# Plain products of ten pairs ahead of their sums in a Strassen-Winograd GeGLU kernel

## The chip, the cores and the metric

The kernel runs on one core of a Trainium2 chip. A core has a matrix engine (TensorE, "PE" in the profile, with its weight loads as "PEld"), a vector engine (VectorE, "DVE"), a scalar engine (ScalarE, "ACT"), a general engine (GpSimd, "POOL") and a queue engine (SyncE, "SP") that issues transfers, as ACT can too. They run side by side and wait for each other by semaphores. Each engine takes its own instructions strictly in order. The metric is the device time of one execution in microseconds; the time given is the median of the runs.

## The reference

```python
def setup_inputs():
    B, S, D, F = 1, 2048, 1024, 3584     # all bfloat16
    ...
def reference(x, w_gate, w_up, w_down):
    return (_gelu(x @ w_gate) * (x @ w_up)) @ w_down    # gelu: tanh form
```

2048 tokens with 1024 features are multiplied by two weight matrices of 1024 x 3584 ("gate" and "up"), GELU of the one is multiplied by the other, and the result goes through a third matrix of 3584 x 1024 ("down").

## The kernel before

**Tiling.** The tokens are taken in two halves of 1024 (`h` = 0, 1), each half in two blocks of 512 (`tb` = 0, 1). The 3584 hidden features are 28 tiles of 128; two neighbouring tiles make a pair, so there are 14 pairs. The contraction over 1024 is 8 steps of 128 (`KD`), in two halves of 4 (`KH`). One matmul multiplies a 128 x 128 weight block by 512 token columns into one PSUM bank of 128 x 512 fp32. There are eight banks, used two by two for gate (`j` = 0) and up (`j` = 1): `PB`, `VB`, `QB`, `RB`.

**Seven products for eight.** Done plainly, a pair needs 2 tiles x 2 blocks x 2 halves of K = 8 products of 4 matmuls, for gate and for up: 64 bf16 matmuls. The kernel uses Winograd's form of Strassen's scheme, seven products, 56 matmuls: M1 and M2 on plain bf16 operands, and M3 to M7 on sums held as fp32r. The sums of x (`t1` to `t4`, `b22`) are made once for a token half by `t_sum`; the sums of weights (`s1` to `s4`, `a22`) are made for each pair by `s_sum` (L388, on POOL; `a22` is a copy on ACT, L401). They have one place per name in `s_mem`, so a sum of the next pair can be made only when the product that reads the old one is over.

**`quads` (from L406)** runs pairs, mostly two at a time (a "couple"). It first does M1 for both pairs (4 matmuls for each of gate and up) and copies M1 to a second bank on ACT (L444), then adds M2 to the first bank: that is the plain output of the pair's first tile on the first token block, and goes through `gelu` (L286, ACT) and `mult` (L291, DVE) into `hT`. Then for each pair, 40 fp32r matmuls:

- M6 on bank Q (which holds M1), copied to bank R on ACT (L478); M5 on bank V, copied to SBUF as `m5` on ACT (L472);
- DVE adds `m5` to Q (L434); M7 goes on R, DVE adds R and `m5` into V (L434); V goes through GELU and product;
- M3 goes on Q, M4 on R, each followed by GELU and product.

`prep` puts the next pair's sums right behind the product that frees their place. `thens` is a table of further work hung between products ("start", "m5", "m7", "m3", "m4").

**Other work hung there in the first token half.** 42 staging steps (`stage_step`, L625, DVE, 128 x 512, SBUF to SBUF) prepare sums of the down weights, which go out to DRAM by SP; transposing loads of the next x (`stage_x`) go on SP; `s_down` (L670, DVE) makes sums of `hT` for the down projection; `t_down` (L600, DVE) makes sums of 1024 columns of the down weights. They stood spread over six couples.

**The start.** Pair 0 is done plainly on both blocks (`first_pair_units`, `part`, L267, 64 matmuls) while the rest of x and the weights land. The first four K steps of x are transposed by TensorE (L311), the others by transposing DMAs. Pair 1 runs alone in `quads` (with "early" in its `thens`: its successor's sums are made late), its own s3 sums on DVE (L386); then come six couples. In the second token half there are seven couples. After each half, `down_group` (L698) runs the down projection on two token groups, also with seven products; its first sums need `s_down` and `t_down` in time.

**Order.** Every instruction is tied to the one before it on its engine by `on`, so the order in the file is the order on each engine.

Of the kernel before, what the change touches and what calls it, by code (L numbers as in the profile page):

```python
# [34 lines left out]
def kernel(  # L35
# [8 lines left out]
    nc = tc.nc  # L44
# [52 lines left out]
    s_mem = shared_pool.tile([P, 4 * NS * P], F32R, name="s_mem")  # L97
# [44 lines left out]

    xs0 = w_mem[:, 4 * CH : 4 * CH + TSB * D].rearrange("p (a b) -> p a b", b=D)
    chunks = {}

    def new_chunk(key):
        c0 = 2 * CH * (key[1] % 2)
        chunks[key] = tuple(
            w_mem[:, c0 + j * CH : c0 + (j + 1) * CH].rearrange(
                "p (a b) -> p a b", b=FG  # L150
            )
            for j in range(2)
        )
# [33 lines left out]
    load_x0(0, sp, 0, 2)  # L187
    load_x0(0, act, 2, TSB)
    load_w(first, 0, 0, 2, sp, 0, FA)
    load_x0(1, act)  # L190
    load_w(first, 1, 0, 2, sp, 0, FA)
    load_w(first, 0, 2, 5, act, 0, FA)
    load_w(first, 1, 2, 5, sp, 0, FA)
# [20 lines left out]
    load_xT(xT, 0, 0, KH, KH + 1)  # L214
    behind_transpose = last_on["sp"]
    load_xT(xT, 0, 0, KH + 1, KH + 2)
    for j in range(2):
        load_w(first, j, 5, KD, act, 0, FA)
        tc.add_manual_dep(
            last_on["act"].ins,  # L220
            behind_transpose.ins.name,
            SCHED_DEP,
            reason="engine order",
        )
    act(nc.scalar.preload_act_table(ACT.Gelu_apprx_tanh))
    load_xT(xT, 0, 0, KH + 2, KD)
    for k0, k1 in ((0, 2), (2, KH), (KH, KD)):
        load_xT(xT, 0, 1, k0, k1)
    for j in range(2):
        load_w(first, j, 0, KD, sp, FA, FG)  # L230
    new_chunk((0, 1))
    for j in range(2):
        load_w((0, 1), j, 0, KD)
# [31 lines left out]
    def mm_gu(ps, w_sb, fi, tb, kd):  # L265
        pe(
            nc.tensor.matmul(  # L267
                ps[:],
                lhsT=w_sb[:, kd, fi * P : (fi + 1) * P],
                rhs=xT[tb][:, kd, :],  # L270
                start=(kd == 0),
                stop=(kd == KD - 1),
            )
        )

# [23 lines left out]
    def unit_out(hT, bset, fi, tb):  # L299
        mult(hT, gelu(banks[bset[0]]), banks[bset[1]], fi, tb)  # L300

    def transpose_x0(q):

        parts = [(2 * q, 0, 4), (2 * q + 1, 0, 4)]
        if q == 0:
            parts = [(0, 0, 2), (0, 2, 4), (1, 0, 4)]
        for n, (kd, ts0, ts1) in enumerate(parts):
            tp = banks[(PB + QB)[(2 * q + n) % 4]][:].bitcast(BF16)
# [14 lines left out]
    def part(held, tb, k0, k1, us=(0, 1), js=(0, 1)):  # L323
        for kd in range(k0, k1):
            for j in js:
                for u in us:
                    mm_gu(banks[held[u][j]], chunks[first][j], u, tb, kd)

    def first_pair_units(hT):

        held = (VB, RB)
        transpose_x0(0)
        warm(RB[1], TB // 2)
        part(held, 0, 0, KPQ, js=(0,))
        transpose_x0(1)
        part(held, 0, 0, KPQ, js=(1,))
        part(held, 0, KPQ, KD)
        t_sum("t1", 0, KH // 2)
        t_sum("t1", KH // 2, KH)
        for u in range(2):  # L340
            unit_out(hT, held[u], u, 0)
        held = (QB, PB)
        part(held, 1, 0, KH)
        t_sum("t2")
        t_sum("b22")
        t_sum("t3", 0, KH // 2)
        part(held, 1, KH, KD, (0,))
        unit_out(hT, held[0], 0, 1)
        t_sum("t3", KH // 2, KH)
        part(held, 1, KH, KD, (1,))  # L350
        unit_out(hT, held[1], 1, 1)
        for j in range(2):
            s_sum(0, 1, j, "s3", True, False)
        for name in ("s1", "s2", "s4"):
            for j in range(2):
                s_sum(0, 1, j, name)
# [5 lines left out]
    def block(key, j, i, kh):  # L362
        fi = 2 * (key[2] % PPG) + i
        w_sb = chunks[(key[0], key[2] // PPG)][j]
        return w_sb[:, half(kh), fi * P : (fi + 1) * P]
# [40 lines left out]
    def quads(hT, h, members, nxt, thens, m5_first):  # L406

        last = nxt is None
        run = []
        for n, pair in enumerate(members):  # L410
            after = (h, members[n + 1]) if n + 1 < len(members) else nxt
            first_ = (PB, RB)[n] if len(members) > 1 else VB
            run.append((pair, after, thens[n], first_, (QB, VB)[n]))
# [27 lines left out]
        for pair, _, _, first_, q_ in run:  # L441
# [4 lines left out]
        for pair, _, _, first_, _ in run:  # L446
# [8 lines left out]
        for n, (pair, after, then, _, Q_) in enumerate(run):  # L455
            f0 = 2 * pair
            ends = after is None
            eager = "early" in then

            def prep(j, name, after=after):  # L460
                if after is not None:
                    s_sum(after[0], after[1], j, name)
# [6 lines left out]
            def do_m5(j):  # L469
# [3 lines left out]
                if not eager:  # L473
                    prep(j, "s1")
# [6 lines left out]
            if eager:  # L481
                order = (do_m5, 0), (do_m5, 1), (do_m6, 0), (do_m6, 1)
            elif m5_first and n == 0:
# [7 lines left out]
            for j in range(2):  # L491
                add_m5(Q_[j], Q_[j], m5[j])
                if not eager:
                    prep(j, "s2")
            done(n, "m5")
            for j in range(2):
# [4 lines left out]
                if j == 0 and eager:  # L501
                    pool_behind_dve()
                    for name in ("s1", "s2"):
                        for i in range(2):
                            prep(i, name)
# [562 lines left out]
```

## Time and profile before

| | |
|---|---|
| median of 3 runs | 538.92 us (538.79 to 539.41) |
| span of the profiled execution | 537.4 us |
| TensorE clock granted | 1.00 throughout |
| POOL sums, L388 | 206 of 1.24, 1.34 and 1.20 us (three forms) |
| DVE steps, L625 from a step before | 28: 0.68 to 1.54 us, median 1.36 |
| DVE additions, L434, with PSUM | 108 of 0.69 us |
| DVE products, L291, with PSUM | 106 of 0.69 us |
| ACT GELU, L286 | 106 of 0.60 us |

The profile is one execution. Its first part gives busy time, share and instructions of each engine; the chain that ended last follows the work back from the last instruction, piece by piece, with start, length and line. A timeline line has start, length, engine, line, operation, tiles and count. "fp32r" and "f32" operands of a matmul are sums, "bf16" ones are plain.

The busy shares in 40 slices of 13.4 us (9 is 90% or more) show where each side engine has work:

```profile
DVE  2985868787876998989555353444444669979961
ACT  2555555556465329117465554656555551452280
POOL 0698696969696200000056494958677670000000
```

The first token half's pairs end at slice 13; slices 13 to 20 are its down projection.

### The profile page before, as it was taken

To read this page: it belongs to the slowest core of one execution; us is meant where nothing else is said; L and a number is where in the kernel's file an instruction comes from. 1 tells how busy PE (TensorE), PEld (TensorE's weight loads), DVE (VectorE), ACT (ScalarE), POOL (GpSimd) and SP (SyncE) were. 2 spreads that over 40 slices of the span, in tenths; PEclk is the share of its full clock that TensorE was granted. 3 is DMA by queue.
4 is the path that set the end of the run, shared out by engine and by line. 5 is a ranking of instruction groups with operands and counts; after the bars stand their busy time and mean duration, and the time that the engine had idled before them with its cause. 6 is when DMAs were issued, how large, how long until landed. Compare 5 with 4: busy or idle time off the path is not lost.

```text
span 537.4 us, 7033 instructions
## 1 busy us (share of the span) xinstructions
PE 533.6 (99%) x2388; PEld 379.2 (71%) x2388; DVE 367.6 (68%) x476; ACT 263.5 (49%) x447; POOL 252.2 (47%) x213
## 2 busy tenths in 40 slices
PE   9999999999999999999999999999999999999997
PEld 4568686867677686777768676776768686866866
DVE  2985868787876998989555353444444669979961
ACT  2555555556465329117465554656555551452280
POOL 0698696969696200000056494958677670000000
PEclk9999999999999999999999999999999999999999
DMA  9965759697623887788950413314040329677846
GB/s 220 329 199 134 267 164 304 182 320 199 229 53 143 318 288 243 243 292 292 329 168 12 145 62 97 110 48 154 3 156 22 136 84 337 228 237 250 292 143 212
DMA packets 92547, 102.70 MB, mean 191 GB/s; under 512 B 18656, under 2 KB 67424, under 8 KB 92512
## 3 DMA queue, kind: packets, MB, share of 16 engines
q1 hardware_dynamic: 69568, 80.23, 45.7%
q10 hardware_dynamic: 22944, 22.02, 13.2%
q8 instruction: 19, 0.31, 0.3%
q14 instruction: 16, 0.13, 0.1%
HBM read 85.98 MB, written 12.58 MB: 183 GB/s over the span
## 4 chain that ended last, share of the span: by engine, by line
PE 99%; ACT 0%; issue 0%
PE bank L418 63%; PE bank L698 33%; PE bank L267 3%; PE bank L202 1%; PE bank L311 0%; ACT o_sb L754 0%
## 5 line engine op out<-in xcount | busy, mean ns | idle before, releaser
L418 PE MATMUL bank<-t_mem,s_mem 128*128 128x512 f32 x1056 | 244.6, 392 | 0.0
L418 PEld LDWEIGHTS bank<-t_mem,s_mem 128*128 128x128 f32 x1056 | 198.1, 188 | 42.7 <-issue 0.2
L388 POOL TENSOR_TENSOR s_mem<-w_mem 128x512 fp32r<-128x512 bf16 x102 | 124.0, 1236 | 185.5 <-DMA out_dram<-o_sb 96.9
L698 PE MATMUL bank<-t_mem,s_mem 128*128 128x512 f32 (+1 forms) x548 | 127.2, 391 | 0.0
L698 PEld LDWEIGHTS bank<-t_mem,s_mem 128*128 128x128 f32 x548 | 102.5, 188 | 22.0
L291 DVE TENSOR_TENSOR hT<-w_mem,bank 128x512 bf16<-128x512 f32 x106 | 72.5, 687 | 66.5 <-PE bank L418 44.5
L434 DVE TENSOR_TENSOR bank<-bank,m 128x512 f32<-128x512 f32 x108 | 70.0, 694 | 56.1 <-ACT m L472 54.3
L418 PE MATMUL bank<-xT,w_mem 128*128 128x512 bf16 x432 | 95.7, 379 | 0.0
L286 ACT ACTIVATE w_mem<-bank 128x512 f32<-128x512 f32 x106 | 63.0, 597 | 64.1 <-DVE bank L434 34.8
L418 PEld LDWEIGHTS <-w_mem 128*128 128x128 bf16 x432 | 41.2, 98 | 51.3 <-issue 3.4
L388 POOL TENSOR_TENSOR s_mem<-w_mem,s_mem 128x512 fp32r<-128x512 bf16 x52 | 68.4, 1335 | 2.9 <-PE bank L418 2.9
L600 DVE TENSOR_TENSOR t_mem<-w_mem 128x1024 fp32r<-128x1024 bf16 x56 | 65.9, 1225 | 0.9 <-PE bank L418 0.9
L388 POOL TENSOR_TENSOR s_mem<-s_mem,w_mem 128x512 fp32r<-128x512 f32 x52 | 61.3, 1200 | 0.0
L401 ACT CAST s_mem<-w_mem 128x512 fp32r<-128x512 bf16 x54 | 33.2, 616 | 31.3 <-PE bank L418 30.1
L478 ACT COPY bank<-bank 128x512 f32<-128x512 f32 x54 | 30.8, 570 | 26.6 <-PE bank L418 26.6
L670 DVE TENSOR_TENSOR s_mem<-hT 128x512 fp32r<-128x512 bf16 x52 | 36.7, 745 | 7.1 <-PE bank L698 7.1
L472 ACT COPY m<-bank 128x512 f32<-128x512 f32 x54 | 31.8, 589 | 18.4 <-PE bank L418 18.4
L698 PEld LDWEIGHTS <-hT 128*128 128x128 bf16 x224 | 21.3, 98 | 26.6 <-issue 2.1
L444 ACT COPY bank<-bank 128x512 f32<-128x512 f32 x54 | 30.7, 570 | 14.3 <-PE bank L418 13.5
L625 DVE TENSOR_TENSOR o_sb<-wd_sb,o_sb 128x512 fp32r<-128x512 bf16 x28 | 32.9, 1176 | 0.5
L763 ACT CAST o_sb<-bank 128x512 bf16<-128x512 f32 x27 | 14.8, 585 | 33.8 <-PE bank L698 33.8
L597 ACT CAST t_mem<-w_mem 128x1024 fp32r<-128x1024 bf16 x28 | 26.9, 1047 | 0.0
(46 smaller groups left out, 236.5 us busy)
## 6 DMA issues: line engine op xcount, KB each, us to landing
t_mem<-t_dram SPq DMA_DIRECT2D x56, 512.0 KB, 5.3
w_mem<-in_w_gate_dram ACTq DMA_DIRECT2D x10, 1024.0 KB, 5.4
w_mem<-in_w_up_dram ACTq DMA_DIRECT2D x10, 1024.0 KB, 8.3
wd_sb<-in_w_down_dram SPq DMA_DIRECT2D x28, 256.0 KB, 5.4
t_dram<-o_sb SPq DMA_DIRECT2D x28, 256.0 KB, 3.5
wd_sb<-in_w_down_dram SPq DMA_DIRECT2D x12, 512.0 KB, 7.6
w_mem<-in_w_down_dram SPq DMA_DIRECT2D x4, 1024.0 KB, 6.7
w_mem<-in_w_down_dram SPq DMA_DIRECT2D x8, 512.0 KB, 8.3
```

What stands on the lines that cost most here:

```text
L286: act(nc.scalar.activation(out=g_sb, in_=ps[:], func=ACT.Gelu_apprx_tanh))
L291: nc.vector.tensor_tensor(out=hT[:, fc, tb * TB : (tb + 1) * TB], in0=g_sb, in1=ps[:], op=ALU.mult,)
L388: pool(nc.gpsimd.tensor_tensor(out=t, in0=in0, in1=in1, op=op))
L401: act(nc.scalar.copy(out=t, in_=a(1, 1)))
L418: nc.tensor.matmul(banks[bank][:], lhsT=lhs[:, c, :], rhs=rhs[:, c, :], start=start and c == 0, stop=c == KH - 1, skip_group_check=True,)
L434: nc.vector.tensor_tensor(out=banks[dst][:], in0=banks[src][:], in1=m5[:], op=ALU.add)
L472: act(nc.scalar.copy(out=m5[j][:], in_=banks[V_[j]][:]))
L478: act(nc.scalar.copy(out=banks[R_[j]][:], in_=banks[Q_[j]][:]))
L600: dve(nc.vector.tensor_tensor(out=t, in0=in0, in1=in1, op=ALU.subtract))
L625: dve(nc.vector.tensor_tensor(out=t, in0=in0, in1=in1, op=ALU.subtract))
L670: dve(nc.vector.tensor_tensor(out=t, in0=in0, in1=in1, op=op))
L698: nc.tensor.matmul(banks[bank][:, c0:c1], lhsT=lhs(i, u), rhs=rhs(i)[:, c0:c1], start=start and i == 0, stop=stop and i == NS - 1, skip_gr ...
```

## The change

The first token half gets another order; the second half is as it was.

- Pair 0 is no longer plain. On the first token block alone, eight tiles (0 to 7, weight chunks 0 and 1) are multiplied plainly at the start, in four sets of two (`first_units`, `plain_products`). Each is the first tile of one pair: `tiles_of` now makes lead pair n of tiles n and 12 + n. When the first half of K is done, the banks hold M1, and `hold` copies them (ACT) as fp32 to `hT` rows and columns not yet in use and to the new `s_late`; the second half of K then completes the plain output.
- Pairs 4 and 5 (tiles 8 to 11, `MID`) run as a couple in the usual way, M1 in banks.
- Then the eight lead pairs run one after the other in `quads` with `plain=False`: no M1 and M2 there; `fetch` copies M1 back from memory into bank Q (ACT), for the next pair behind M7. Each is 40 fp32r matmuls.
- In these ten pairs, the next pair's s3 sums are made by DVE (`s3_dve`) and not by POOL.
- The staging steps are hung anew: 5 in the couple, 20 in the leads (one at each start, one or two by turns at M3), 17 in the two couples that follow; the late s3 sums of the down projection go behind M4 in the leads' end and in these couples. The x transposes and stores move to the leads' middle and to the couples.
- Weight chunks 0 and 4 lie in `hT` until those rows are used; chunks 3 to 5 come in halves on ACT's queue (`load_half`). `s_mem` is smaller, and the last sums of the down projection go to `s_late`.

```diff
+    LEADS = (0, 1, 2, 3, 6, 7, 8, 9)
+    MID = (4, 5)
+    LOW = NL + 2 * len(MID)
+    def tiles_of(h, pair):
+        if h == 0 and pair in LEADS:
+            return LEADS.index(pair), LOW + LEADS.index(pair)
+        return 2 * pair, 2 * pair + 1
...
+    for j, queue in enumerate((sp, act)):
+        load_x0(0, queue, ts.start, ts.stop)
+        load_w(first, j, 0, KPQ, queue, 0, FA)
+        load_x0(1, queue, ts.start, ts.stop)
+        load_w(first, j, 0, KPQ, queue, FA, FG)
+        load_w(first, j, KPQ, KH, queue)
...
+    load_xT(xT, 0, 0, KH, KD)
+    for f0 in (FA, 0):
+        for j in range(2):
+            load_w(first, j, KH, KD, sp, f0, f0 + FA)
+    new_chunk((0, 1))
...
+    def hold(held, tiles, j):
+        for u, t in enumerate(tiles):
+            act(nc.scalar.copy(out=p_hold(t, j), in_=bank2(held[u][j])))
...
+        top(0, 0, 0, KPQ)
+        top(0, 1, 0, KPQ)
+        transpose_x0(1)
+        top(1, 0, 0, KPQ)
+        top(0, 0, KPQ, KH)
+        top(0, 1, KPQ, KH)
+        top(1, 1, 0, KPQ)
+        top(1, 0, KPQ, KH)
+        top(1, 1, KPQ, KH)
+        outs(*rest(1))
+        outs(*rest(0))
...
-    def quads(hT, h, members, nxt, thens, m5_first):
+    def quads(hT, h, members, nxt, thens, m5_first, plain=True, s3_dve=False):
...
+        def fetch(n):
+            for j in range(2):
+                act(nc.scalar.copy(out=bank2(run[n][4][j]), in_=p_hold(n, j)))
...
+        if not plain:
+            fetch(0)
...
                 if after is not None:
-                    s_sum(after[0], after[1], j, name)
+                    on_dve = s3_dve and name == "s3"
+                    s_sum(after[0], after[1], j, name, on_dve, False)
...
+            if not plain or (m5_first and n == 0):
                 order = (do_m5, 0), (do_m6, 0), (do_m6, 1), (do_m5, 1)
...
+            if not plain and n + 1 < len(run):
+                fetch(n + 1)
             done(n, "m7")
...
+            quads(hT, h, MID, (h, LEADS[0]), thens, False, True, True)
+            thens = [{} for _ in LEADS]
+            for n in range(NL):
+                thens[n]["start"] = [lambda: run_steps(1), run_loads]
+                thens[n]["m3"] = [lambda n=n: run_steps(1 + n % 2), run_loads]
+            for n in range(NL // 2):
+                thens[2 + n]["start"].append(run_x)
+            thens[1]["start"].append(lambda: load_half(4, 0))
+            thens[3]["start"].append(lambda: load_half(4, FA))
...
+            quads(hT, h, LEADS, (h, begin), thens, True, False, True)
...
+                add(0, "m1", lambda: run_steps(4), run_loads)
+                if lead < NPAIR - PPG:
+                    add(0, "start", lambda: run_steps(3))
+                add(1, "start", lambda: run_steps(1))
                 for n in range(PPG):
                     add(n, "start", run_loads, run_x)
-                    add(n, "m7", store_x, run_loads)
+                    add(n, "m4", store_x, run_loads)
                     add(n, "m3", lambda: run_steps(1), run_loads)
+                    add(n, "m4", run_late)
```

In the changed kernel `mult` is L305, `gelu` L300, `s_sum` on DVE L447 and on POOL L449, the matmuls of `quads` L481, the additions of `m5` L497, the R copies L542, `fetch` L476, the plain products L342, the staging steps L685 and the sums of the down weights L660.

## The prediction

> **What bounds the kernel now.** I read the totals first, then the chain that ended last, then the timeline of VectorE (DVE) and GpSimd (POOL) inside one couple.
>
> ```profile
> PE 533.6 (99%) x2388; PEld 379.2 (71%) x2388; DVE 367.6 (68%) x476; ACT 263.5 (49%) x447; POOL 252.2 (47%) x213
> ```
>
> ```profile
> 6.87 12.95 PE bank L267 x60
> 19.82 163.21 PE bank L418 x728
> 183.03 87.89 PE bank L698 x392
> 270.92 175.56 PE bank L418 x784
> 446.48 87.95 PE bank L698 x396
> ```
>
> The chain is TensorE without a break: only matmul work removed from it, or a wait put into it, can change the time. It also gives the prices. The plain bf16 matmuls (L267) run at 12.95/60 = 0.2158 us. The second token half is 784 matmuls in 175.56 us: 224 bf16 ones take 48.34 us of it, so the 560 fp32r ones run at 127.22/560 = 0.2272 us. A couple of pairs takes 175.56/7 = 25.08 us.
>
> ```profile
> 80.00:100.00 20.00, 20.00 (x91) 13.89 (x90) 16.65 (x21) 11.15 (x20) 14.77 (x13) 1.00 0.85 274
> ...
> 82.90 0.68 DVE L291 TENSOR_TENSOR hT<-w_mem,bank 128x512 bf16<-128x512 f32 x1
> 83.50 1.04 DVE L625 TENSOR_TENSOR o_sb<-wd_sb 128x512 fp32r<-128x512 bf16 x1
> 84.57 3.10 DVE L625 TENSOR_TENSOR o_sb<-wd_sb,o_sb 128x512 fp32r<-128x512 bf16 x2
> 87.59 0.68 DVE L625 TENSOR_TENSOR o_sb<-wd_sb 128x512 fp32r<-128x512 bf16 x1
> ...
> 83.95 3.17 POOL L388 TENSOR_TENSOR s_mem<-w_mem,s_mem 128x512 fp32r<-128x512 bf16 x2
> ```
>
> The first row is the stage table (columns after the stretch: PE, PEld, DVE, ACT, POOL busy): DVE is busy 16.65 of 20 us, so it has slack, but not much. The timeline rows show its price list. An L625 step alone takes 0.68 us and lets the next start after 0.60. Beside a POOL sum it takes 1.04 (met half way) or 1.55 (held for all of it, starts 1.51 apart), and POOL's sums stretch too, to 1.58 from 1.17. Operations that read PSUM (L291, L434) stay at 0.68 to 0.70, also 0.60 apart.
>
> **The change, part by part.**
>
> *Removed.* Pair 0 was 64 plain matmuls; it becomes 16 plain and 40 fp32r. 48 x 0.2158 = 10.36 us go and 40 x 0.2272 = 9.09 us come: -1.27 us on the bound itself. Everything else on TensorE only moves.
>
> *Moved to the front.* 128 plain matmuls (27.6 us) now need all of weight chunks 0 and 1 and half of x, in place of half a chunk and all of x. The second half of the K range of pair set 1 starts after some 12.7 us and needs 2.62 MB by then. The stage table of before has 171, 257 and 226 GB/s in the first three stretches of 5 us: 0.86 + 1.29 + 0.61 = 2.75 MB by 12.7 us. I take no DMA wait; if it is missed, see the rivals.
>
> *Added on ACT.* 16 copies of M1 out of PSUM as fp32 (nearest row L472, 589 ns) lie behind plain products of the other sets, two per 1.73 us; I take 0.09 us, bounds 0 and one copy, 0.59. 16 copies back (`fetch`) are SBUF fp32 to PSUM, which no row has; L444 (570 ns) and L401 (616 ns) bound them, I take 0.62. A lead pair then has about 5.5 us of ACT in 9.09 us: hidden. The exception is the first fetch: it stands in ACT's order behind the last GELU and the last a22 cast of the couple. Counted from lead 0's start, they end at +0.32 and +0.84, the fetch at +1.46; from the end of a releasing instruction to the matmul I charge 0.16 us (0.05 is seen between an L478 copy and the weight load behind it, 0.11 is an estimate between 0 and the 188 ns of an L418 weight load). M6 should start at +0.91 and starts at +1.62: **0.71 us**.
>
> *The lead pairs on DVE.* This is the expensive part. A pair used to share a couple of 112 matmuls with 25.08 us; a lead pair has only its 40 sums' products, 40 x 0.2272 = 9.09 us. DVE has to do, in each, 4 additions and 3 products from PSUM (7 x 0.60 = 4.2 us), the two s3 sums taken over from POOL, and by turns 2 or 3 staging steps: 9 SBUF operations in two leads. At 0.60 alone and 1.51 held that is 13.8 to 22.0 us of DVE in 18.2 us. POOL has six sums a lead, 6 x 1.17 = 7.0 of 9.09 us, so most of the nine meet one.
>
> Take a lead that follows one with two steps at its M3; zero is its start, -4.55 the end of the lead before's first M7 product. DVE adds M5 to the up half of Q until -4.0, then does add V, s3, add V, s3, product V, product Q, step, step, product R. That is 5 x 0.60, two s3 met half way (0.96 each, as the 1.04 us row) and two steps held (1.51 each): -4.0 + 3.0 + 1.92 + 3.02 = +3.94. The result is there 0.09 later, ACT copies the next R out of it (0.05 + 0.57), and M7's second product, due at 20 x 0.2272 = 4.54, starts at 4.81: 0.27 us. DVE's next are a held step and the addition to Q that M3 needs: 3.94 + 1.51 + 0.60 + 0.09 + 0.16 = 6.30, due at 5.45 + 0.27: 0.58 us. So **0.85 us**, three times (leads 2, 4, 6): 2.55. Behind each wait stand all of TensorE's products and, on ACT, GELU and the next casts; POOL, whose six sums wait for TensorE to have read the old ones, waits with it. A lead after one with a single step is 1.51 us earlier and makes both dates. Bounds for the round: all SBUF operations alone end product R at +1.4, no wait; all held, +5.2, waits of 1.5 and 0.6, with 0.6 in the other leads too.
>
> *The ends of the row of leads.* The couple behind it needs the R banks at 12 x 0.2158 = 2.59 us; product R comes after one held step and one alone, -4.0 + 3.0 + 1.92 + 1.51 + 0.60 = 3.03, plus 0.17: **0.61**. In the couple before, three steps round the pair border make its M3 wait 0.21, and the first plain products wait 0.13 for products behind t sums.
>
> *Into the down projection.* 17 of the 42 steps are left for two couples, which also carry the late s3 sums. In the last pair DVE's order before the addition that M3 needs is product R (ends +1.1), late sum 0.60, step 1.5, t1 sum of 1024 columns (1.22 alone in the L600 rows, 2.1 held), addition 0.60: +5.97 plus 0.25, due at 5.45: **0.77**. In before, no step and no late sum stand there. What is still late makes one t1 or s2 sum of M5 late: 0.33, an estimate from the same lag.
>
> *Queues.* The half chunks 3 to 5 go on ACT's queue (0.38 to 0.54 us an issue, L160 rows) with slack; SP's stage loads, stores and transposes stay in DVE's order, and land behind it. No wait is charged; a missed one costs DVE, as above.
>
> *Sum:* -1.27 + 2.55 + 0.71 + 0.21 + 0.61 + 0.77 + 0.33 + 0.09 + 0.13 = **+4.1 us**. The profiled execution spans 537.4 us, 1.5 below the median of 538.92; these 1.5 us lie around the span and stay. Forecast: 541.5 span, **543.1 us**, slower.
>
> One rule speaks to the price of a meeting. The rows have two held steps starting 1.51 us apart, against 0.60 alone. The Trainium skill (SBUF — State Buffer, section "Who interferes with whom") has DVE and GpSimd lock a shared port pair, the second waiting until the first's whole instruction is done; a two-input addition from SBUF meets GpSimd's reads in this way. By that a held step would last the POOL sum's 1.17 and its own 0.60, 1.77 us; the trace shows less, so the lock seems to be let go before the sum's end. With 1.77 the three held steps of an even lead would end 3 x 0.26 = 0.8 us later, and the sum be about 545.5.
>
> **Rivals.**
>
> *DVE keeps its dates.* If no more than two of the five SBUF operations between -4.0 and M3's date meet a sum, DVE ends at -4.0 + 11 x 0.60 + 2 x 0.91 = +4.4, in time. Then the leads, their end and the couple cost nothing and the first fetch, 0.71, stays: -1.27 + 0.71 = -0.6, 538.4; if ACT is earlier than I count, -1.27, 537.65. For it: the median of the 14 first steps of before (L625 from two bf16 inputs) is 686 ns. Against it: POOL is busy 7 of 9 us.
>
> *The other leads wait too.* A step more held in the leads after a single step puts their addition behind M3's date by 0.6: 4 x 0.6 = 2.4 on top, 545.5. For it: the 1.58 us sums of POOL, which lengthen its own row. Against it: whenever TensorE waits, POOL runs dry first and DVE catches up.
>
> *The start waits for weights.* 2.62 MB at the lowest of the three rates from 5 us on is 12.8 us; with one or two transfers queued behind the transposing DMA, up to 2 us late: 545.1. Against it: the 512 byte pieces of before become 1024 byte ones in part.
>
> That the change doesn't do what it says can be left out: the built order has 8 fewer matmuls.
>
> **How the numbers follow.** Forecast 0.70; DVE in time 0.12; other leads too 0.10; late start 0.08. The forecast's own range is 541 to 545.3; both slower rivals end near its top, so 540.5 to 546.0 leaves out the faster rival and the tails, some 0.2. This measurement can tell 0.2%, 1.1 us: faster needs all waits under 0.2 us, 0.06; within, 0.07; slower, 0.87.
>
> **What would show it.** Right: breaks in the matmuls of L481 in every second lead, just under a microsecond together, ended by ACT's R copy (L542) and DVE's addition (L497); L685 steps and L447 sums at 1.0 to 1.6 us; one break of 0.7 us before the first lead; bf16 and fp32r paces unchanged. Wrong: TensorE unbroken from 60 to 138 us and DVE idle between its operations; or breaks ended by DMA in the first 15 us.

## The result, and the profile after

| | before | after |
|---|---|---|
| median, same chip | 539.04 us (538.79 to 539.41, 4 runs) | 544.65 us (543.92 to 546.09, 4 runs) |
| ratio | 1 | 1.0107 [1.0090, 1.0124] |
| profiled execution: time, span | 537.4 us span | 543.92 us, 542.1 us span |

The changed kernel is slower by 5.6 us in the medians and by 4.8 us between the two profiled spans (537.35 and 542.14 us in the traces). The granted clock is 1.00 in both. The totals of the changed kernel:

```profile
PE 534.5 (99%) x2380; PEld 381.1 (70%) x2380; DVE 385.3 (71%) x498; ACT 272.8 (50%) x471; POOL 246.3 (45%) x202
```

There are the 8 matmuls fewer, and 22 VectorE operations more, so the change does what it says. TensorE's share says nothing of the loss: it is still 99%. The chain that ended last does (start, length, what):

```profile
7.03 25.93 PE bank L342 x120
32.95 21.44 PE bank L481 x96
...
59.16 0.50 ACT bank L476
59.66 0.14 issue
59.79 15.68 PE bank L481 x68
...
83.44 11.16 PE bank L481 x48
...
102.58 11.16 PE bank L481 x48
...
121.71 11.16 PE bank L481 x48
...
163.72 7.53 DMA x_dram<-hT
171.26 0.02 issue
171.28 0.70 DVE hT L305
...
196.75 7.70 DMA t_mem<-t_dram
204.46 0.14 issue
204.59 70.92 PE bank L758 x315
275.52 175.56 PE bank L481 x784
```

Before, five unbroken rows of TensorE made up this chain from 6.87 us on. Now TensorE gives it away between 59 and 205 us: to a fetch on ACT, to VectorE once in every second lead, and to two transfers. The three rows of 48 matmuls start 19.14 and 19.13 us apart; two leads are 80 x 0.2272 = 18.18 us of matmuls, so 0.96 is lost each time. From 275 us on nothing has changed: the second half's 784 matmuls take 175.56 us as before.

The matmuls' starts in the trace give the full balance. A break is the time from one matmul's start to the next beyond its pace, its place is the start of the first of the two, and leads are counted from 0:

| place | break, us | forecast | ended by |
|---|---|---|---|
| start, to 33 us | 0 (before: 0.77) | 0.09 | |
| first plain product of the middle couple | 0 | 0.13 | |
| border inside the middle couple, 54.0 | 0.35 | 0.21 | DVE, ACT |
| first fetch, 58.9 | 0.72 | 0.71 | ACT L476 |
| leads 2, 4, 6 (81, 100, 120) | 0.96, 0.96, 0.96 | 3 x 0.85 | ACT L542, DVE L497 |
| end of the leads, 136.9 | 0.58 | 0.61 | DVE L305 |
| last couple, 171.4 and 173.5 | 1.19 and 0.33 | none | DMA `x_dram<-hT`, then ACT |
| last pair's M3 | 0 | 0.77 | |
| down projection, 203.8 | 0.63 | 0.33 | DMA `t_mem<-t_dram` |

The breaks add up to 6.68 us. With -1.27 for the matmuls and -0.85 for before's own breaks (0.77 at its start, 0.08 at 119.9 us) that is +4.56; the last matmul starts 538.73 - 534.14 = 4.59 us later.

One lead's break, shortened (start, length, engine, line, operation, tiles, shapes, count; in brackets the idle time and what ended it):

```profile
75.75 2.75 POOL L449 TENSOR_TENSOR s_mem<-hT,s_mem 128x512 fp32r<-128x512 bf16 x2
...
77.45 1.60 DVE L685 TENSOR_TENSOR o_sb<-wd_sb,o_sb 128x512 fp32r<-128x512 bf16 x1
...
78.45 1.62 POOL L449 TENSOR_TENSOR s_mem<-w_mem 128x512 fp32r<-128x512 bf16 x1
78.97 1.65 DVE L685 TENSOR_TENSOR o_sb<-wd_sb 128x512 fp32r<-128x512 bf16 x1
...
80.55 0.67 DVE L305 TENSOR_TENSOR hT<-w_mem,bank 128x512 bf16<-128x512 f32 x1
80.98 1.16 POOL L449 TENSOR_TENSOR s_mem<-w_mem 128x512 fp32r<-128x512 bf16 x1 [0.91 <-PE bank L481]
81.14 1.55 DVE L685 TENSOR_TENSOR o_sb<-wd_sb,o_sb 128x512 fp32r<-128x512 bf16 x1
81.31 0.57 ACT L542 COPY bank<-bank 128x512 f32<-128x512 f32 x1 [1.56 <-DVE hT L305]
...
81.93 0.77 PEld L481 LDWEIGHTS bank<-t_mem,s_mem 128*128 128x128 f32 x4 [0.55 <-ACT bank L542]
...
82.61 1.88 DVE L497 TENSOR_TENSOR bank<-bank,m 128x512 f32<-128x512 f32 x3
83.44 3.89 PE L481 MATMUL bank<-t_mem,s_mem 128*128 128x512 f32 x16 [0.32 <-DVE bank L497]
```

DVE goes from one operation to the next without a gap: two steps, the product that frees bank R (80.55), a third step, and only then the addition that M3 needs (82.61). ACT's R copy waits 1.56 us for the product; TensorE waits for the copy first, then for the addition.

### The profile page after: what moved, and what is told of

Same layout as the page of the kernel before. It is cut to its first block, busy times and chain, and to the rows that moved or that the text cites. A ratio compares the mean times of both kernels' runs of the same rounds, so it can differ in the third digit from the quotient of the medians.

```text
span 542.1 us, 7109 instructions
## 1 busy us (share of the span) xinstructions
PE 534.5 (99%) x2380; PEld 381.1 (70%) x2380; DVE 385.3 (71%) x498; ACT 272.8 (50%) x471; POOL 246.3 (45%) x202
## 4 chain that ended last, share of the span: by engine, by line
PE 90%; DVE 4%; DMA 3%; issue 2%; ACT 1%; SPq 0%; DVEq 0%; ACTq 0%
PE bank L481 53%; PE bank L758 31%; PE bank L342 5%; DVE o_sb L685 2%; DMA t_mem<-t_dram 1%; DMA x_dram<-hT 1%; DVE hT L305 1%; PE bank L232 1%; DVE bank L497 0%; SPq L709 0%; PE bank L324 0%; ACT w_mem L300 0%; ACT bank L542 0%; ACT bank L507 0%; DVE xT L332 0%
## 5 line engine op out<-in xcount | busy, mean ns | idle before, releaser
L481 PE MATMUL bank<-t_mem,s_mem 128*128 128x512 f32 x1096 | 254.7, 392 | 2.9 <-ACT bank L542 0.9
L481 PEld LDWEIGHTS bank<-t_mem,s_mem 128*128 128x128 f32 x1096 | 205.0, 188 | 50.0 <-POOL s_mem L449 2.7
L449 POOL TENSOR_TENSOR s_mem<-w_mem 128x512 fp32r<-128x512 bf16 x80 | 97.1, 1232 | 190.3 <-DVE t_mem L287 99.3
L305 DVE TENSOR_TENSOR hT<-w_mem,bank 128x512 bf16<-128x512 f32 x106 | 71.2, 683 | 69.8 <-PE bank L481 39.5
L497 DVE TENSOR_TENSOR bank<-bank,m 128x512 f32<-128x512 f32 x112 | 72.7, 692 | 42.7 <-ACT m L537 41.0
L758 PE MATMUL bank<-t_mem,s_mem 128*128 128x512 f32 x416 | 98.4, 394 | 0.4 <-DMA t_mem<-t_dram 0.4
L300 ACT ACTIVATE w_mem<-bank 128x512 f32<-128x512 f32 x106 | 62.6, 596 | 60.7 <-DVE bank L497 39.0
L758 PEld LDWEIGHTS bank<-t_mem,s_mem 128*128 128x128 f32 x416 | 78.0, 188 | 17.8 <-DVE t_mem L660 0.8
L481 PE MATMUL bank<-xT,w_mem 128*128 128x512 bf16 x320 | 71.0, 379 | 0.4 <-DVE hT L305 0.4
L660 DVE TENSOR_TENSOR t_mem<-w_mem 128x1024 fp32r<-128x1024 bf16 x56 | 65.7, 1218 | 0.4 <-PE bank L481 0.4
L449 POOL TENSOR_TENSOR s_mem<-w_mem,s_mem 128x512 fp32r<-128x512 bf16 x46 | 61.2, 1352 | 3.4 <-PE bank L481 3.4
L481 PEld LDWEIGHTS <-w_mem 128*128 128x128 bf16 x320 | 30.6, 98 | 38.5 <-issue 3.0
L449 POOL TENSOR_TENSOR s_mem<-s_mem,w_mem 128x512 fp32r<-128x512 f32 x46 | 57.3, 1265 | 0.2
L542 ACT COPY bank<-bank 128x512 f32<-128x512 f32 x56 | 31.9, 571 | 29.6 <-PE bank L481 20.4
L685 DVE TENSOR_TENSOR o_sb<-wd_sb,o_sb 128x512 fp32r<-128x512 bf16 x28 | 30.4, 1086 | 0.3
L758 PE MATMUL bank<-t_mem,s_late 128*128 128x512 f32 (+1 forms) x132 | 30.3, 382 | 0.0
L507 ACT COPY bank<-bank 128x512 f32<-128x512 f32 x40 | 22.8, 570 | 12.6 <-PE bank L481 12.6
L730 DVE TENSOR_TENSOR s_mem<-hT 128x512 fp32r<-128x512 bf16 x36 | 23.5, 686 | 7.0 <-PE bank L758 7.0
```

The lines of the kernel that those rows point to most:

```text
L300: act(nc.scalar.activation(out=g_sb, in_=ps[:], func=ACT.Gelu_apprx_tanh))
L305: nc.vector.tensor_tensor(out=hT[:, fc, tb * TB : (tb + 1) * TB], in0=g_sb, in1=ps[:], op=ALU.mult,)
L449: pool(nc.gpsimd.tensor_tensor(out=t, in0=in0, in1=in1, op=op))
L481: nc.tensor.matmul(banks[bank][:], lhsT=lhs[:, c, :], rhs=rhs[:, c, :], start=start and c == 0, stop=c == KH - 1, skip_group_check=True,)
L497: nc.vector.tensor_tensor(out=banks[dst][:], in0=banks[src][:], in1=m5[:], op=ALU.add)
L542: act(nc.scalar.copy(out=banks[R_[j]][:], in_=banks[Q_[j]][:]))
```

## The experiments

All ratios are to the kernel before on the same chip. The kernel before took 538.78 to 539.35 us on the chips of these runs, so medians of two runs that differ by less than some 0.6 us are better compared by their ratios. No run leaves out any computation.

| run | median, us | ratio, 95% interval |
|---|---|---|
| s3 sums of the leads all on POOL | 551.55 | 1.0222 [1.0204, 1.0240] |
| three of four s3 sums on DVE | 541.81 | 1.0053 [1.0039, 1.0066] |
| rows late | 544.22 | 1.0094 [1.0080, 1.0108] |
| fetch early | 545.15 | 1.0111 [1.0098, 1.0125] |
| two steps in each lead | 544.90 | 1.0111 [1.0097, 1.0124] |
| three of four, rows late | 542.01 | 1.0052 [1.0039, 1.0064] |
| three of four, rows behind the stores | 541.59 | 1.0044 [1.0031, 1.0057] |
| the same, and fetch early, one step moved | 541.04 | 1.0038 [1.0025, 1.0052] |
| the same, and the start's order | 540.98 | 1.0033 [1.0020, 1.0045] |
| the same, and two sums moved | 540.68 | 1.0025 [1.0015, 1.0034] |
| the same, and one step later | 539.62 | 1.0008 [0.9999, 1.0017] |
| changed kernel, the start's order alone | 544.97 | 1.0107 [1.0094, 1.0121] |

**Is it VectorE, and where else can the work go?** First the s3 sums, which the change had moved from POOL to VectorE.

```diff
-            quads(hT, h, LEADS, (h, begin), thens, True, False, True)
+            quads(hT, h, LEADS, (h, begin), thens, True, False, False)
```

> All s3 sums of the eight leads go back from VectorE to POOL; nothing is left out. Theory A (VectorE is full in the leads: of two leads it owes 14 PSUM operations x 0.60, 4 sums x 0.94 and 5 staging steps x about 1.5, near 19.7 us beside 18.18 of quads): the three breaks of 0.29 + 0.11 and 0.49 + 0.08 at the even leads go, worth 2.9 us. But POOL then makes eight sums a lead, 8 x 1.17 = 9.4 unheld and up to 8 x 1.6 = 12.8 held, against 9.09 of quads, so POOL becomes the bound and the time ends 1 to 6 us above the changed kernel, at 545.5 to 550.5. Rival B (the breaks come from ScalarE's R copy, and where the s3 sum is made doesn't matter): breaks as before the edit, 544 to 545. Rival C (POOL keeps up): breaks gone and nothing in their place, 541.5 to 542.

551.55 us. Theory A's sign and place hold: in the stage table of two pairs of leads (columns after the stretch: PE, PEld, DVE, ACT and POOL busy, clock, DMA share, GB/s) POOL is busy for 20.17 and 18.75 us, where two leads' matmuls last 18.18, and DVE has room:

```profile
74.30:94.60 20.30, 18.41 (x81) 14.93 (x81) 15.55 (x20) 11.79 (x24) 20.17 (x17) 1.00 0.53 157
94.60:116.00 21.40, 19.82 (x81) 15.88 (x80) 14.55 (x20) 11.76 (x23) 18.75 (x17) 0.92 0.52 141
...
96.00:98.00 2.00, 2.00 (x6) 1.58 (x5) 1.40 (x3) 1.44 (x3) 2.00 (x2) 0.50 1.20 282
```

Four breaks of 1.8 to 2.1 us stand where three of 0.96 stood, in leads 1, 3, 5 and 7, and all four come about in one way:

```profile
90.96 1.61 POOL L449 TENSOR_TENSOR s_mem<-hT,s_mem 128x512 fp32r<-128x512 bf16 x1
...
92.61 0.42 ACTq L190 DMA_DIRECT2D hT<-in_w_up_dram  x1
93.13 0.58 ACT L537 COPY m<-bank 128x512 f32<-128x512 f32 x1 [3.54 <-POOL s_mem L449]
93.61 1.08 ACT L542 COPY bank<-bank 128x512 f32<-128x512 f32 x2
...
94.34 5.03 PE L481 MATMUL bank<-t_mem,s_mem 128*128 128x512 f32 x14 [1.89 <-ACT bank L542]
```

At the start of these leads ACT issues a half-chunk load (L190) that overwrites weights which a late sum on POOL still reads. ACT waits for the sum, and its M5 and R copies stand behind the issue. So POOL's lateness reaches TensorE by way of the loads in ACT's order; what it would cost with the loads on another queue was not run.

B and C fall. The time is above the expected range because of something no theory had: the clock of 0.50 in the third row, taken up at the end; it cost two times 1.6 us, without which the profiled run's 552.33 would be 549.1. One of the four runs, with a mean clock of 0.999, took 549.73, inside the range. So the eight sums of a lead do not fit POOL, and moving some to VectorE was needed; how many is the question.

```diff
-                    on_dve = s3_dve and name == "s3"
+                    on_dve = s3_dve and name == "s3" and (plain or j == 0 or n % 2 == 0)
```

> Of each two leads' four s3 sums one goes back to POOL (the second sum made in an odd lead); nothing is left out. Theory A (VectorE full): its load of two leads falls by 0.94 to about 18.7 us, POOL's rises by one sum to 13 of about 1.3, near 17 of 18.18; the breaks at 81, 100 and 120 us shrink from 0.95 to under 0.35 each, and the median ends 1.8 to 2.9 us below the changed kernel's 544.65, at 541.7 to 542.9. Rival B (ScalarE's R copy, as such, is late): the 0.29 + 0.11 in front of the Q addition stays in each even lead, gain at most 1.7. Rival D (the pairs' meetings of a POOL sum with a VectorE step make the time, not VectorE's total): a sum more on POOL means as many meetings or more, breaks as large as now, 544 to 545.

541.81 us, inside theory A's range: the breaks of the leads and of their end went from 2.88 + 0.58 us to four pieces of 0.06 to 0.11. B and D fall. Two pairs of leads, the changed kernel's first and this run's second:

```profile
64.30:83.40 19.10, 18.70 (x82) 14.83 (x80) 18.80 (x23) 11.89 (x22) 17.31 (x13) 1.00 0.48 144
83.40:102.50 19.10, 18.69 (x80) 14.86 (x80) 18.39 (x24) 11.93 (x22) 16.60 (x13) 1.00 0.65 180
```

```profile
63.30:81.50 18.20, 18.20 (x82) 15.08 (x81) 17.79 (x24) 11.98 (x22) 17.14 (x13) 1.00 0.53 174
81.50:99.80 18.30, 18.30 (x82) 14.93 (x81) 17.83 (x23) 11.88 (x22) 18.02 (x14) 1.00 0.69 175
```

In the changed kernel DVE needs 18.4 to 18.8 us in leads whose matmuls last 18.18; one sum moved to POOL, and both engines fit, DVE with 17.8 and POOL with 18.0 at most.

Then the dose: more steps in the leads.

```diff
-                thens[n]["m3"] = [lambda n=n: run_steps(1 + n % 2), run_loads]
+                thens[n]["m3"] = [lambda: run_steps(2), run_loads]
```

> The changed kernel with two staging steps at M3 in every lead, the even ones too, so four steps more in the eight leads and four fewer in the couples behind; nothing is left out. Theory A (VectorE full): its load of two leads goes from 19.7 to about 21.2 beside 18.18 of quads, each two leads' break of 0.95 grows by 1.0 to 1.6, in four places: 548 to 551, less up to 0.6 where the couples have fewer steps. Rival D (the breaks are the cost of single meetings at fixed places, not of the total): breaks of 0.95 as now, or one more such break a lead, 544 to 546.5.

544.90 us: theory A's number is wrong by some 3 us, and D's holds it. There are four breaks, of 0.96, 0.96, 0.97 and 1.54 us: one more, and only the last larger. Yet the stage table, from break to break, shows VectorE's total at work:

```profile
75.00:93.90 18.90, 18.49 (x80) 14.71 (x80) 18.83 (x24) 11.78 (x22) 16.73 (x13) 1.00 0.63 181
94.00:113.20 19.20, 18.77 (x81) 14.78 (x80) 19.13 (x26) 11.78 (x22) 16.96 (x13) 1.00 0.63 192
```

DVE has no idle time left at all (18.83 of 18.90, 19.13 of 19.20), so it is the bound there, but its load did not grow by a held step. From one step's start to DVE's next operation the trace has a mean of 1.41 and 1.22 us in the changed kernel's two stretches, 1.17 in these. The reason is in the rows: four of these twelve steps start before the POOL sum that they meet and take 0.68 us, and the sum waits; in the changed kernel's two stretches it is one of ten. So A's price falls: its load of 19.7 us for the changed kernel was made with held steps; measured it is 18.4 to 18.8. Its mechanism rests on the run before this one and on the stage tables; this run's time alone would speak for D.

**The wait for a transfer at 171 us.** The x stores (L709, 128 KB each) are issued at 162.9 to 164.7 us and land at 171.1 to 172.2, behind two 1 MB loads of down-weight rows (L603, issued 161.2 and 161.9, landed 166.8 and 170.1). The change had moved these loads from the start of pair 12 to pair 11. From the changed kernel's timeline:

```profile
161.23 1.07 SPq L603 DMA_DIRECT2D w_mem<-in_w_down_dram  x2
...
162.94 2.37 SPq L709 DMA_DIRECT2D x_dram<-hT  x4
...
171.28 0.69 DVE L305 TENSOR_TENSOR hT<-w_mem,bank 128x512 bf16<-128x512 f32 x1 [1.98 <-DMA x_dram<-hT]
172.06 0.57 ACT L542 COPY bank<-bank 128x512 f32<-128x512 f32 x1 [3.20 <-DVE hT L305]
...
172.77 1.15 PE L481 MATMUL bank<-t_mem,s_mem 128*128 128x512 f32 x4 [0.94 <-ACT bank L542]
```

The four stores behind the loads take 7.5 to 8.2 us from issue to landing. The median of all eight stores is 5.5 us, and was 1.8 before.

```diff
-                if pair == NPAIR - 2 - (h == 0):
+                if pair == NPAIR - 2:
...
-                        "start" if h else "m7",
+                        "start",
```

> The two loads of down-weight rows go back to the start of pair 12, behind the x stores of pair 11; nothing is left out. Theory A (the break of 1.19 at 171 us is the small x store waiting in its ring behind two 1 MB loads): the store lands within 3 us of its issue, the break goes, and nothing of it is left: 1.0 to 1.3 us below the changed kernel, 543.3 to 543.7. Rival B (the 0.77 forecast for VectorE at that pair's M3 was real and only masked): a break of 0.4 to 0.8 appears within 3 us of that place, gain 0.2 to 0.6. Rival C (the rows come too late for the right-hand sums of the down phase): a new wait behind 180 us, no gain or a loss.

544.22 us. The break at 171 is gone and so is the 0.33 behind it, but this is not theory A's gain. In the last pair (this run's timeline) a new one of 0.83 stands:

```profile
181.83 2.19 DVE L660 TENSOR_TENSOR t_mem<-w_mem 128x1024 fp32r<-128x1024 bf16 x1
183.95 2.48 DVE L497 TENSOR_TENSOR bank<-bank,m 128x512 f32<-128x512 f32 x4
184.78 1.39 PE L481 MATMUL bank<-t_mem,s_mem 128*128 128x512 f32 x5 [0.59 <-DVE bank L497]
```

The addition to Q stands behind a 2.19 us sum of down weights on DVE. That is rival B in kind, one pair later than it was put: the 0.77 that was forecast for this very place was real, and in the changed kernel the transfer's delay had given DVE the time to catch up. So by the break it is B, and the median, 0.43 us less, is in B's range. The profiled execution can't be read by its span: it waited for weights at 7.8 us and behind them at 36.8, and came 2.4 us later than the changed kernel's to the couple's later products.

With three of four s3 sums on DVE the same edit did no better.

> The run with three of four s3 sums on VectorE, and the down-weight rows loaded at the start of pair 12 again as in the kernel before; nothing is left out. Theory A (in the run with only the rows late, 1.19 at 171 us went and 0.83 came at 183.8, in the last pair's Q addition behind a down-phase operation L660 on VectorE: the gap went from the DMA ring to VectorE): the 1.01 at 169.0 goes, 0.7 to 0.9 comes in the last pair, and the down phase starts no earlier: 541.0 to 541.8 beside 541.81. Rival B (the 0.83 was VectorE's lag left over from the eight leads, which are lighter now): no break in the last pair, and the 1.0 is gained whole: 540.4 to 540.9.

542.01 beside 541.81 us. The 1.01 at 169 us went and 0.83 came in the last pair, theory A's exchange; the median is 0.2 above its range, with one more break of 1.12 in the leads at 119 us in the profiled execution. B falls: the lag there isn't a rest of the leads'.

The next run keeps the loads in pair 11, but issues them behind the stores.

```diff
-                        "start" if h else "m7",
+                        "start" if h else "m4",
...
-                add(
-                    n,
-                    "start",
+                thens[n].setdefault("start", [])[:0] = [
                     lambda: load_b22(4, NS),
```

> Three of four s3 sums on VectorE; the two rows loads issued in pair 11 but behind its four x stores instead of ahead of them; in the last pair the five weight loads are issued ahead of that pair's staging step instead of behind it. Nothing is left out. Theory A (a small store waits for the megabytes issued ahead of it in the same ring, and the down phase's start at 189.2 waits 1.11 for loads issued only once a step's store has been): the 1.01 + 0.32 at 169 go, the 1.11 falls to 0.5 or less, and as the rows still land before pair 12 is over, nothing comes in their place: 540.0 to 540.8. Rival B (VectorE's 0.8 in the last pair stands behind it, as where the rows were late): 540.8 to 541.5. Rival C (the x stores' own readers make the wait, not the order in the ring): no change at 169, 541.4 to 542.2.

541.59 us: theory A on the ring is right, its time is missed, and B's by 0.1. The stores' median from issue to landing (tiles, queue, count, KB each, us) is down to 2.4 us, and the four that had stood behind the loads take 1.9 to 2.2:

```profile
x_dram<-hT SPq DMA_DIRECT2D x8, 128.0 KB, 2.4
```

The breaks at 169 and 189 us are gone, with nothing but the order in one queue changed; C falls. But B's 0.83 in the last pair came, and a break of 0.78 in the down projection (226 us, `t_mem<-t_dram`), which no theory had.

**The first fetch.**

```diff
-        if not plain:
-            fetch(0)
...
+            if s3_dve and plain and n == len(run) - 1:
+                for j in range(2):
+                    act(nc.scalar.copy(out=bank2(QB[j]), in_=p_hold(0, j)))
             done(n, "m7")
```

> The first lead's two halves are fetched into their banks behind the last couple's third product of the second pair, not behind its end; nothing is left out. Theory A (0.72 at 58.9 is one copy that PE waits for, but VectorE is already late behind it): the 0.72 goes and VectorE's lateness shows instead within the next two leads, 0.4 to 1.1 us: between 0.3 below and 0.4 above the changed kernel. Rival B (the fetch alone made the wait): 0.6 to 0.8 below, 543.9 to 544.0.

545.15 us, 0.1 above theory A's upper end; B falls. The 0.72 at 58.9 us is gone and 1.02 stands at 63.7, ended by DVE: three steps lie between 59.4 and 64.1 us. The next run adds this to the run with the rows behind the stores; one of the three steps is taken out and put into the fifth lead's M3.

> The run before this one, and: the first fetch behind the last couple's third product, the staging step at the last M4 of the second pair of the middle couple taken out and put into the fifth lead's M3 (two there). Nothing is left out. Theory A (where only the fetch was moved, 0.72 was replaced by 0.94 of VectorE, three steps in a row between 59.4 and 64.1 us; with one of them gone VectorE keeps up): 0.5 to 0.8 less than the run before it, 539.4 to 540.2, beside 539.34 of the kernel before. Rival B (VectorE's lag only moves on into the leads that follow): a break of 0.4 to 0.9 between 64 and 110 us, gain 0 to 0.3.

541.04 us, 0.55 less than the run with the rows behind the stores. Nothing waits between 56 and 90 us any more, as A has it; but 0.99 stands at 109 us, at the start of the sixth lead, right behind the step's new place, which is B's. The gain is A's, 0.5 to 0.8; A's absolute range is missed by 0.8, as the run that it started from had missed its own.

**The start.** In the profiled execution of the changed kernel TensorE never waits before 33 us. In six of the eight other profiles with this start it does, at 7.4 to 8.4 us, for the second weight blocks (L190): they land at 7.4 and 8.2 us in the changed kernel's profile, at 9.3 and 9.5 in that of the run with the rows late.

```diff
         top(1, 0, 0, KPQ)
+        top(1, 1, 0, KPQ)
         top(0, 0, KPQ, KH)
         top(0, 1, KPQ, KH)
-        top(1, 1, 0, KPQ)
```

> The changed kernel with one step of its start in another place: the four plain products of the second tile pair's up half (first two row blocks) come ahead of, not behind, the first pair's products that need the next weight blocks; nothing is left out. Theory A (these weight blocks, loads L190 issued at 3.1 to 4.0 us, landed at 7.4 us in the changed kernel's profile and at 7.7 to 9.5 in six others, where TensorE waited for them 0.3 to 1.6 us at 7.4 to 8.4; this makes the changed kernel's runs spread over 2.2 us and its median lie 0.7 above its profiled run): 4 x 0.216 = 0.86 of the wait is covered, the median falls by 0.4 to 0.8 to 543.8 to 544.3, and the runs spread less. Rival B (the spread comes from elsewhere, the steps in the leads or the transfers behind them): no change, 544.4 to 545.0. Rival C (TensorE then waits for the two banks of the transposes): a new wait of 0.2 to 0.6 at 7.9.

544.97 us: by the median, B. The wait at 7.4 us is gone from the profile, though the blocks landed at 8.2 and 8.4; but 0.48 stands at 35.6 us instead, at the middle couple's first plain products. The runs spread over 1.1 us and not over 2.2; with four runs each that is no more than a hint.

> The run with four parts undone or mended (three of four sums, rows behind stores, fetch, one step moved), and the start's order as in the other run of this call; nothing is left out. Theory A: 0.4 to 0.8 below its 541.04, at 540.2 to 540.7, still 1.4 to 1.9 above the kernel before, because VectorE is left with 0.75 in the last pair, some 0.8 in the leads and 0.35 at the middle couple's border, which eat the 1.27 that the sums save. Rival B: no change, 540.8 to 541.3.

540.98 us: no change of the median, B. But the kernel before was 0.57 us slower on this run's chip than on that of the run it is compared with; by the ratios some 0.3 us are gained, which the intervals do not tell from nothing.

**The last pair, and one step later.**

```diff
-        t_sum("t3", KH // 2, KH)
         t_sum("b22")
         outs(*rest(3))
+        t_sum("t3", KH // 2, KH)
...
-                add(n, "m6", lambda: t_down(0, "t1", 4, 6))
+                add(n, "m7", lambda: t_down(0, "t1", 4, 6))
```

> As the run before it, with the down phase's first right-hand sum moved from behind the last pair's M6 to behind its M7, and the second half of one token sum behind the fourth plain unit's outputs; nothing is left out. Theory A (VectorE owes the work all the same): the 0.75 + 0.08 in the last pair goes but 0.4 to 0.9 comes in the first product of the down phase, and the 0.1 to 0.5 at 36 us goes: 0 to 0.5 below the run before it. Rival B (the place alone made the wait): 0.8 to 1.3 below, 539.2 to 539.7, which would be the level of the kernel before.

540.68 us, 0.30 less, theory A, in size and in place: the 0.83 in the last pair is gone, and 0.5 comes at the down projection's first products (192 to 195 us), in five pieces of 0.09 to 0.11, each behind a weight load that waits for a sum of down weights on DVE. Besides, 0.66 at 225 us waits for `t_mem<-t_dram`, which A didn't have. The largest left is 0.98 at 108 us. The last run moves the step that makes it:

```diff
-                thens[n]["m3"] = [lambda n=n: run_steps(2 if n in (1, 3, 4, 5, 7) else 1), run_loads]
+                thens[n]["m3"] = [lambda n=n: run_steps(1 + n % 2), run_loads]
...
-                add(1, "start", lambda: run_steps(1))
+                add(1, "start", lambda n=2 if lead < NPAIR - PPG else 1: run_steps(n))
```

> As the run with six parts, with one of the two staging steps at the fifth lead's M3 moved to the start of pair 11, where that run's trace has no break between 140 and 192 us; nothing is left out. Theory A (the 0.76 + 0.11 at 108.6 is three steps in a row, 105.1 to 109.8 us, in front of the R copy that a gate or up product must free first, and the couple behind has room): the break goes, nothing over 0.3 comes at 150 to 160: 0.5 to 0.9 below 540.68, at 539.8 to 540.2, still 0.4 to 0.9 above the kernel before. Rival B (VectorE owes the work wherever it stands): the break comes again within the leads or in the couple, 540.4 to 541.0.

539.62 us (539.37 to 540.01, 11 runs), 1.06 less: theory A, a little beyond its range. The chain of this run:

```profile
33.62 21.43 PE bank L481 x96
55.04 0.10 issue
55.15 77.12 PE bank L481 x337
```

The leads' matmuls are one row, with no break above 0.11 us. The ratio to the kernel before is 1.0008 [0.9999, 1.0017]: about all of the loss is undone, and nothing is gained. The last matmul starts 0.38 us later than before's (534.51 against 534.14), so this run's breaks are 1.27 + 0.38 = 1.65 us longer than before's 0.85, 2.5 us in all. To be read are 0.40 at the start, 0.26 for a hold at 12.5, 0.35 in the middle couple, three of 0.06 to 0.11 in the leads, 0.29 at 153, and six of 0.06 to 0.11, 0.6 together, at the down projection's first products from 192 to 195 us, where DVE's sums of down weights are late again; the rest, some 0.3, is in pieces too small to read, in a trace that lacks 20 matmul records.

## Why the prediction was right, and where it was not

*The matmul price: right.* 48 bf16 and 40 fp32r matmuls at 0.2158 and 0.2272 us, -1.27; the paces are unchanged in the balance above.

*The leads on DVE: right in mechanism and place, 13% small.* Breaks in leads 2, 4 and 6, ended by the R copy and then by the addition; 0.96 each for 0.85. The R copy made the difference: 0.40 for 0.27 at the first of the two, 0.57 for 0.58 at the second. The run with one s3 sum back on POOL shows the cause by taking it away; the run with all back on POOL shows that the change had to put some there.

*Held steps: the price right, the reason given for it wrong.* The three steps in the timeline above start 1.52, 1.58 and (to the addition) 1.47 us apart, for 1.51 in the sum. The prediction concluded from such distances that POOL lets the lock go before its sum ends. The ends of the rows say otherwise: the POOL sums end at 78.50, 80.07 and 82.14 us, the steps that met them at 79.05, 80.62 and 82.69, each 0.55 us later. All 46 steps and s3 sums on DVE in the changed kernel's trace that start while a POOL sum runs end 0.54 to 0.56 us after that sum. With this the trace agrees with the rule of the Trainium skill (SBUF — State Buffer, section "Who interferes with whom"), that the second waits for the whole of the first's instruction. The 1.77 us charged a whole sum of 1.17, but a held step starts when the sum is already under way, here by 0.13, 0.52 and 0.16 us. That the measured median lies between 543.1 and 545.5 doesn't speak for the 1.77: the leads cost 0.33 us more than forecast, not 2.4.

*First fetch and the leads' end: right,* 0.72 and 0.58 for 0.71 and 0.61. The fetch's price was right, its worth was not separate: taken away alone, DVE's lag of 1.02 us stood behind it.

*"No wait is charged" for the queues: wrong.* This is the step that failed, and the largest miss. SP's order was followed for the steps' stores, but the two rows loads of 1 MB that the change pulls ahead of four x stores were not weighed: a store of 128 KB then waits for 2 MB ahead of it, and the product that overwrites its source waits for it on DVE. Price 1.19 and 0.33 behind it. The runs with the rows late and behind the stores both take it away.

*The last pair, 0.77: right, but hidden.* It didn't show in the changed kernel, as the transfer's break came first; without that it was 0.83.

*Into the down projection, 0.33: wrong in kind and size.* The break is 0.63, and it ends with a load of staged sums from DRAM, issued at 196.75 and landed at 204.46 behind a row of others. The last step's store was issued at 188.7; in before all such stores were out by 158.3, and the first of these loads went at 181.2 against 189.1 us. The change put the steps later, and the loads that need them came later too.

*The start: right in the profiled execution, not in general.* No break there; in the profiles of the eight runs with the same start the middle couple's first matmul comes 0.2 to 1.6 us later, 0.8 in the mean. The late start was a rival. Of the 1.55 us between forecast and median, 0.82 lie between the forecast and the profiled execution, 0.73 between that and the median. It suggests itself that the 0.73 are this start, but it stays open: where one of its waits was taken away, the median stayed.

Together: 4.1 forecast; 1.52 for the stores, 0.30 for the down projection, 0.33 for the leads and 0.14 for the couple's border more, 0.77, 0.13 and 0.09 less, and 0.85 of before's own breaks that the sum had left in, make 4.56. That forecast and balance lie only 0.5 us apart is in part luck: 1.82 us of waits for transfers that were not charged, or not enough, stand against 0.77 that one of them hid and 0.85 that the sum should have taken off.

## What to carry to other kernels

When matmuls are taken away from a stretch, ask which engine has the next largest total in that stretch, with the durations of that stretch: here 18.2 us of TensorE had 18.4 to 18.8 of VectorE beside it, and one sum of 0.9 to 1.0 us moved to another engine in each two leads was worth 2.8 us over the eight leads. Ask also which loads an engine issues: in the run with all s3 sums on POOL, ACT's copies waited because a load in front of them had to wait. A break that goes may uncover the next one's lateness: three of the mends here brought back 0.8 to 1.0 us elsewhere until the steps behind them were moved as well. And when a big transfer is moved to an earlier place, look at the small ones that now stand behind it in its queue, and at who waits to overwrite their source.

## What the runs showed of the hardware

In the run with all s3 sums on POOL, two breaks of 2.05 and 2.00 us (start to start 2.28 and 2.23) were followed by seven matmuls at 0.427 us with a half slow one on either side before the pace was 0.227 again: the granted clock was 0.50 from 95.64 to 99.06 us and from 136.60 to 140.02, 3.41 us each, and some 1.6 us were lost each time. Two breaks of 1.77 and 1.74 us in the same run were not followed by any. In idle time of TensorE these are 1.89 and 1.84 us against 1.60 and 1.58. The two slow stretches start 40.96 us apart, twelve times 3.41; counted in steps of 3.41 us from them, each of the four waits lies whole within one step, so in this run the length of the wait made the difference, and not its place in the step. The Trainium skill (TensorE: Matmul & The Clock Gate, section "Part 1: The HAM clock gate (the "warmup" mystery)") has the clock halved after an idle window of about 3.4 us; the length of the slow stretch, 3.41 us, agrees, but here waits of 1.84 and 1.89 us were enough.

A staging step's price is no constant, but it can be told from the trace: 0.68 us when no POOL sum runs at its start (the next starts after 0.60), else what is left of the sum and 0.55. A sum that finds a step running ends 1.01 to 1.04 us after that step, and takes up to 1.63 us for 1.16. In the leads the mean from a step to the next operation was 1.41 and 1.22 us in the changed kernel and 1.17 where VectorE had more to do. And four stores of 128 KB took 7.5 to 8.2 us from issue to landing behind two 1 MB loads in their queue, 1.9 to 2.2 ahead of them.
